# A bank of its own for value products, a new program order with two split chunks, and a scheduler that prices changes of array use, in an attention and MoE kernel

## The chip, the core and the metric

One core of one Trainium2 chip runs the program. Its engines work side by side: TensorE (PE) for matmuls, whose weights are loaded by PEld rows, VectorE (DVE), ScalarE (ACT), GpSimd (POOL) and SyncE (SP), which here issues every DMA. The metric is the device time of one execution in microseconds (us), lower is better.

## The reference

```python
scores = scale * np.matmul(q, k.transpose(0, 1, 3, 2))      # q, k, v: 4 x 8 x 576 x 64
scores = np.where(causal, -1000000000.0, scores)
a = np.exp(scores - scores.max(-1, keepdims=True))
a /= a.sum(-1, keepdims=True) + 1e-09
local = np.matmul(a, v)
q_p = phi(q)                                                # elu(q) + 1
mem_out = (q_p @ M_prev) / (q_p . z_prev + 1e-6)
attn = g * mem_out + (1 - g) * local                        # g = sigmoid(beta) by head
x = attn as 2304 tokens x 512
h = x @ w_in                                                # 512 x 2048
g = h where h >= 1, 0 where h <= -1, else (h + 1)**2 / 4
out = g @ w_out                                             # 2048 x 512
```

## The kernel before

Attention comes in 16 units of two heads; two units are a pair. Each pair is loaded by `load` (L281) and prepared by `prep` (L314): every operand is split into an fp16 high and low part, so that each product is three matmuls (`PASSES`). `half_a` does the first 256 query rows of a unit and `half_b` the other 320. Each takes score tiles (`front`, L436: scores at L415, the causal mask added by a matmul with the identity at L418, row maxima on DVE at L462, exponentials on ACT at L432), scales them (`back`: `an` tiles, high part by ACT, low part by DVE at L116), has them transposed by DMA (`ea`, `eb`, `ec`) and multiplies with the values (`pv1`, `pv2`, L533). Score matmuls use 64 of the array's rows, value products 64 of its columns, all else the whole array.

The MLP runs in 9 chunks of 256 tokens over 8 weight groups of 256 hidden columns. A group of a chunk is 24 matmuls of 256 columns into a tile h (`mlp_h`, L648), five steps that turn h into g (ACT L653 reads h, ACT L654 squares, DVE L655 reads h again and is the last to do so, then ACT L109 and DVE L116 write g's two halves), and 12 matmuls of 512 columns that add to a tile o (`mlp_o`, L665). `weight_group` (L177) makes the two halves of a weight group from 64-bit words, by DVE at L201 to L203 and L116.

PSUM has eight banks: `RINGS` gives two score tiles of two banks (s), one o of two, and two h of one. Value products take a score tile too, and the first units' scores take the o tile at times (`s_tile`).

`PROGRAM` is the order in which the source emits its parts: l loads a pair, P prepares it, W makes a weight group, A and B are the halves of units, p splits a chunk's input, c runs a chunk; `c0/2,5` cuts the first chunk's groups into three passes with a partial sum in `part`. `in_order` then sorts all instructions for each engine: `estimate` prices each, `listed` runs a list schedule forward and backward 24 times, and the best order is fixed.

Of the kernel before, what the change touches and what calls it, by code (L numbers as in the profile page):

```python
# [25 lines left out]
RINGS = dict(x=3, rq=1, rk=1, rn=1, rv=1, rm=2, rz=2, pn=1, eb=1, ec=1, ea=1, st=4, sc=3, wss=4, wssb=4, g=3, tm=4, part=1,  # L26
    tb=3, tu=3, s=2, o=1, h=2, xsc=3)
# [22 lines left out]
def infini_moe_kernel(ctx: ExitStack, tc, qt, kt, qr, vr, mem, zx, beta, w, out):  # L50
# [86 lines left out]
    wrs = const.tile([P, NG], F32, name="wrs")  # L137
    wirs = const.tile([P, NG], F32, name="wirs")
# [39 lines left out]
    def weight_group(r):  # L178
# [8 lines left out]
        for m in range(2):  # L187
# [17 lines left out]
            words.append(wt)  # L205
        kind(job, "wn")
# [227 lines left out]
    def front(u, i):  # L434
# [23 lines left out]
        for t, a in tiles:  # L458
            scores(u, t, s, a)
# [136 lines left out]
    def chunk_prep(c):  # L596
# [11 lines left out]
        hx, sx, rs, irs = (sc[:, j:j + 1] for j in (2, 3, 4, 5))  # L608
# [395 lines left out]
```

## Time and profile before

| | us |
|---|---|
| median of 3 runs | 643.14 (639.9 to 644.32) |
| the profiled execution | 640.85 |
| its span, first to last instruction | 639.0 |
| PE busy, of the span | 532.7 |
| DVE busy | 483.4 |
| ACT busy | 456.3 |

A slice of the profile's second part is a fortieth of the span, some 16 us; a digit is the busy share in tenths. A matmul's duration holds its latency too, so a busy PE row says that work was there, while the distance from one start to the next says what a matmul costs in a stream.

### The profile page before, as it was taken

How to read it: one execution, taken by the hardware profiler on the slowest of the kernel's cores; microseconds unless marked ns; L12 is line 12 of the kernel's file. 1: busy time of each engine (PE TensorE's matmuls, PEld its weight loads, DVE VectorE, ACT ScalarE, POOL GpSimd, SP SyncE). 2: the span in 40 equal slices, each digit the busy share in tenths (PEclk: the TensorE clock that was granted, in tenths of full speed). 3: DMA queues.
4: the chain of work that ended last, by engine and by line, in shares of the span. 5: the costliest groups of instructions: out<-in, count | busy, mean ns of one | idle time of the engine just before them, and what ended most of it. 6: DMA issues, size and time to landing. Idle time of an engine off the chain costs nothing.

```text
span 639.0 us, 11689 instructions
## 1 busy us (share of the span) xinstructions
PE 532.7 (83%) x4481; PEld 333.5 (52%) x4481; DVE 483.4 (76%) x1134; ACT 456.3 (71%) x916; POOL 2.4 (0%) x12
## 2 busy tenths in 40 slices
PE   0332546673678999999999999999999999999997
PEld 0111224442444666566565656656556566666764
DVE  5999999999999976987978689877667556424321
ACT  5866757959797877797987879788866565644443
POOL 1000000000000000000000000000000000000000
PEclk9999998967678999999999999999999999999999
DMA  7787686766745443692395337613533444000000
GB/s 301 248 288 219 182 208 181 197 184 164 135 112 141 104 77 70 133 216 68 76 196 83 73 93 143 139 25 74 97 72 49 81 84 58 34 1 1 33 1 34
DMA packets 133351, 74.68 MB, mean 117 GB/s; under 512 B 122800, under 2 KB 124848, under 8 KB 131248
## 3 DMA queue, kind: packets, MB, share of 16 engines
q1 hardware_dynamic: 133296, 73.94, 48.7%
q8 instruction: 35, 0.57, 0.4%
q14 instruction: 20, 0.16, 0.1%
HBM read 38.80 MB, written 4.72 MB: 68 GB/s over the span
## 4 chain that ended last, share of the span: by engine, by line
PE 69%; DVE 20%; DMA 4%; ACT 3%; issue 3%; SPq 1%; ACTq 0%; DVEq 0%
PE o L665 28%; PE h L648 27%; PE s L533 6%; PE s L415 4%; DVE an L116 3%; DMA eb<-an 2%; DVE st L462 2%; DVE w L202 2%; DVE w L203 1%; PE s L418 1%; DVE w L116 1%; PE s L443 1%; DMA rm<-mem 1%; DVE w L201 1%; DVE vs L116 1%
## 5 line engine op out<-in xcount | busy, mean ns | idle before, releaser
L648 PE MATMUL h<-xh,w 128*128 128x256 f16 x1728 | 221.7, 279 | 9.4 <-ACT xh L109 4.1
L665 PE MATMUL o<-w,g 128*128 128x512 f16 x864 | 212.8, 384 | 0.5 <-DVE part L694 0.5
L648 PEld LDWEIGHTS <-w 128*128 128x128 f16 x1728 | 169.2, 100 | 56.0 <-issue 17.0
L665 PEld LDWEIGHTS <-g 128*128 128x128 f16 x864 | 82.0, 99 | 83.0 <-issue 8.0
L432 ACT ACTIVATE e<-s,st,sc 128x512 f32<-128x512 f32 (+4 forms) x140 | 89.3, 640 | 20.7 <-DVE st L428 10.6
L655 DVE SCALAR_TENSOR_TENSOR tm<-h,tb,tm 128x512 f32<-128x512 f32 x72 | 53.6, 747 | 60.4 <-ACT tm L654 59.7
L653 ACT ACTIVATE tm<-h,tb 128x512 f32<-128x512 f32 x72 | 55.8, 776 | 53.4 <-PE h L648 49.3
L116 DVE SCALAR_TENSOR_TENSOR an<-e,st,an 128x512 f16<-128x512 f32 (+4 forms) x160 | 80.8, 540 | 7.6 <-ACT an L109 7.3
L109 ACT ACTIVATE g<-tm,tb 128x512 f16<-128x512 f32 x72 | 51.8, 722 | 32.3 <-DVE tm L655 30.3
L116 DVE SCALAR_TENSOR_TENSOR g<-tm,tb,g 128x512 f16<-128x512 f32 x72 | 53.6, 746 | 18.5 <-ACT g L109 18.3
L415 PE MATMUL s<-ks,qs 64*128 64x512 f16 (+3 forms) x372 | 45.8, 331 | 25.1 <-ACT e L432 16.4
L462 DVE TENSOR_REDUCE st<-s 128x2 f32<-128x768 f32 (+3 forms) x62 | 51.1, 829 | 19.9 <-PE s L418 16.6
L109 ACT ACTIVATE an<-e,st 128x128 f16<-128x128 f32 (+3 forms) x112 | 55.1, 541 | 15.0 <-issue 5.4
L533 PEld LDWEIGHTS <-vs 128*64 128x64 f16 x1024 | 40.1, 119 | 32.2 <-issue 30.7
L654 ACT ACTIVATE tm<-tm 128x512 f32<-128x512 f32 x72 | 45.3, 631 | 1.1
L415 PEld LDWEIGHTS <-qs 64*128 64x128 f16 x384 | 16.1, 100 | 45.4 <-issue 32.8
L533 PE MATMUL s<-pt,m 128*64 128x256 f16 (+1 forms) x184 | 18.7, 271 | 12.0 <-DMA pt<-pn 4.5
L432 ACT ACTIVATION_READ_ACCUMULATOR e<-s,st,sc 128x1 f32 x140 | 27.8, 198 | 0.0
L309 PE MATMUL s<-sc,ones 128*128 128x4 f32 (+1 forms) x32 | 6.1, 260 | 22.9 <-ACT m L330 18.8
L533 PE MATMUL s<-eb,vs 128*64 128x256 f16 (+1 forms) x384 | 23.6, 268 | 1.9 <-DMA eb<-an 1.9
L476 DVE SCALAR_TENSOR_TENSOR st<-st,cg 128x2 f32<-128x2 f32 (+2 forms) x64 | 10.0, 157 | 16.2 <-ACT e L432 16.1
L109 ACT ACTIVATE w<-w,wsc 128x1024 f16<-128x1024 f32 x15 | 17.2, 1146 | 7.0 <-DVE w L116 6.9
(161 smaller groups left out, 599.8 us busy)
## 6 DMA issues: line engine op xcount, KB each, us to landing
stg<-w SPq DMA_DIRECT2D x16, 1024.0 KB, 5.6
rv<-vr SPq DMA_DIRECT2D x7, 640.0 KB, 5.7
out<-tm SPq DMA_DIRECT2D x16, 256.0 KB, 2.1
rn<-qr SPq DMA_DIRECT2D x7, 576.0 KB, 4.3
rk<-kt SPq DMA_DIRECT2D x7, 576.0 KB, 3.9
rq<-qt SPq DMA_DIRECT2D x7, 576.0 KB, 4.8
rz<-zx SPq DMA_DIRECT2D x16, 96.0 KB, 4.4
rm<-mem SPq DMA_DIRECT2D x16, 64.0 KB, 3.0
```

What stands on the lines that cost most here:

```text
L109: return nc.scalar.activation(o, i, AF.Copy, scale=s)
L116: nc.vector.scalar_tensor_tensor(o, i, s, hi, op0=ALU.mult, op1=ALU.subtract)
L202: nc.vector.scalar_tensor_tensor(wti, hw, -0x40000000, wti, op0=ALU.bitwise_and, op1=ALU.bitwise_or)
L415: nc.tensor.matmul(s[:, h, a:a + n], u.pair.q[hs, tq, u.x, i * P:(i + 1) * P], u.pair.k[hs, tk, u.x, 0:n], start=j == 0, stop=False)
L432: nc.scalar.activation(e, s, AF.Exp, bias=st[:, 0, z:z + 1], scale=u.pair.cs, accum_out=st[:, 1, z:z + 1])
L462: nc.vector.tensor_reduce(st[:, 0, 2 * t:2 * t + 2], s[:, :, a:a + P * (t + 1)], axis=AX.X, op=ALU.max, negate=True)
L533: nc.tensor.matmul(pv[h * D:(h + 1) * D, a:c1], lhs, rhs, start=n < 2, stop=n >= len(terms) - 2)
L648: nc.tensor.matmul(h[:, u], w1[:, r, cc, wj, u * P:(u + 1) * P], x16[:, xj, cc, :], start=n == 0, stop=n == 3 * NCC - 1)
L653: nc.scalar.activation(tm, h, AF.Relu, bias=tb[:, 1, j:j + 1], scale=tb[:, 2, j:j + 1])
L654: nc.scalar.activation(tm, tm, AF.Square)
L655: nc.vector.scalar_tensor_tensor(tm, h, tb[:, 0, j:j + 1], tm, op0=ALU.max, op1=ALU.min)
L665: nc.tensor.matmul(acc[:, t], g16[:, gj, u, t * P:(t + 1) * P], w2[:, r * FPG + u, wj, :], start=(r == a and u == 0 and gj == 0 and wj == ...
```

## The change

It has these parts, with the lines of the new source.

- Value products: `pv1` and `pv2` write a one-bank tile `v` of their own; scores always take s, no longer o; h has one bank in place of two (`RINGS`).
- `front` of the first two query tiles issues both tiles' scores and then all four masks.
- `PROGRAM`: the first four units' attention comes before most weight groups; chunks 0 and 1 are each cut after group 4 (`c0/4`, `c1/4`); `part` has two buffers.
- `load`: z joins q's rows and M joins v's rows in DRAM, so a pair is four DMAs in place of eight, and q's rows are loaded first.
- `tables`: one DVE product by a broadcast in place of three.
- The scheduler: `listed` keeps three queues for PE, by the array's use, adds `TURN` (95 ns) where the use changes, and stays with a use while its first instruction is no more than `KEEP` (1500 ns) less urgent.

```diff
-RINGS = dict(x=3, rq=1, rk=1, rn=1, rv=1, rm=2, rz=2, pn=1, eb=1, ec=1, ea=1, st=4, sc=3, wss=4, wssb=4, g=3, tm=4, part=1,
-    tb=3, tu=3, s=2, o=1, h=2, xsc=3)
+RINGS = dict(x=3, rq=1, rk=1, rn=1, rv=1, pn=1, eb=1, ec=1, ea=1, st=4, sc=3, wss=4, wssb=4, g=3, tm=4, part=2,
+    tb=3, tu=3, s=2, o=1, h=1, v=1, xsc=3)
...
-PROGRAM = ("l0 l1 P0 W0 A0 P1 W1 A1 A2 W2 A3 p0 c0/2,5 W3 B0 W4 c0 B1 W5 l2 B2 W6 P2 B3 W7 c0 l3 p1 A4 A5 P3 c1 "
-           "A6 l4 A7 p2 B4 B5 P4 c2 B6 l5 B7 p3 P5 c3 A8 A9 A10 l6 A11 p4 B8 B9 P6 c4 B10 l7 B11 p5 P7 c5 A12 "
-           "A13 A14 A15 p6 B12 B13 c6 B14 B15 p7 c7 p8 c8")
+PROGRAM = ("l0 l1 P0 W0 A0 A1 P1 A2 A3 p0 W1 B0 W2 B1 W3 c0/4 B2 B3 p1 W4 l2 c1/4 W5 W6 W7 c0 c1 P2 A4 A5 l3 P3 "
+           "A6 A7 l4 p2 B7 B4 B5 P4 c2 l5 B6 A9 p3 P5 c3 A8 l6 A10 A11 p4 B8 B9 P6 c4 B10 B11 l7 p5 P7 c5 A12 "
+           "A14 A15 A13 B13 p6 B14 c6 B15 B12 p7 c7 p8 c8")
...
-        for c, t, src in (("lk", u.kt, kt), ("lq", u.qt, qt), ("lr", u.qr, qr), ("lv", u.vr, vr)):
+        for c, t, src in (("lr", qz1, qz), ("lk", u.kt, kt), ("lq", u.qt, qt), ("lv", vm1, vm)):
             kind(u.job, c)
             nc.sync.dma_start(out=t, in_=src[p])
-        kind(u.job, "lm")
-        for h in range(2):
-            hs = slice(h * D, (h + 1) * D)
-            nc.sync.dma_start(out=u.mf[hs], in_=mem[p])
-            nc.sync.dma_start(out=u.zf[hs], in_=zx[p, h:h + 1].to_broadcast([D, 2, 3, D]))
...
-        tag = next(spare) if u.n < 4 and u.n not in late else "s"
+        tag = "s"
...
-        for h in range(2):
-            nc.tensor.matmul(s[:, h, a + n - P:a + n], ident, mask, start=False, stop=True)
...
-            scores(u, t, s, a)
+            scores(u, t, s, a, a == 0)
+        for t, a in tiles:
+            for h in range(2):
+                nc.tensor.matmul(s[:, h, a + P * t:a + P * (t + 1)], ident, mask, start=False,
+                                 stop=t == tiles[-1][0])
...
-        pv = s_tile(u, f"pv1{u.n}")[:, 0]
+        pv = ps.tile([P, 512], F32, name=f"pv1{u.n}", tag="v")
...
-        nc.vector.tensor_scalar(t[:, 0, 0:n], wsc[:, 0, a:b], sx, None, op0=ALU.mult)
-        nc.vector.tensor_scalar(t[:, 1, 0:n], wrs[:, a:b], rs, None, op0=ALU.mult)
-        nc.vector.tensor_scalar(t[:, 2, 0:n], wirs[:, a:b], irs, None, op0=ALU.mult)
+        nc.vector.tensor_tensor(t[:, 0:3, 0:n], wtb[:, :, a:b], xtb.unsqueeze(2).to_broadcast([P, 3, n]), op=ALU.mult)
...
+TURN, KEEP = 95.0, 1500.0
...
+            pick = min(a[0] for a in alike if a)
+            if alike[use] and alike[use][0][0] <= pick[0] + KEEP:
+                pick = alike[use][0]
+            k = pick[1]
+            heapq.heappop(alike[mode[k]])
+            if mode[k] != use:
+                at += TURN
+            use = mode[k]
```

How the instructions stand now, at three places. Names end in a buffer's number: w1 and w2 are the weights' halves, stg a staging tile, an the scaled probabilities, tm and g the steps after h.

DVE, while the last weight groups are made. Before, with the low half of the seventh group's input weights (w1 from w2) in the middle:

```order
L116 SCALAR_TENSOR_TENSOR an_0_239<-e_0_234,st_0_214,an_0_239 128x128 x2
L116 SCALAR_TENSOR_TENSOR an_0_239<-e_0_234,st_0_214,an_0_239 128x2x128
L116 SCALAR_TENSOR_TENSOR m1_0_138<-rm_0_87,sc_2_1233,m1_0_138 128x256
L116 SCALAR_TENSOR_TENSOR g_1_590<-tm_1_589,tb_0_548,g_1_590 128x512
L116 SCALAR_TENSOR_TENSOR w1_73<-w2_74,wsc_77,w1_73 128x4x256
L116 SCALAR_TENSOR_TENSOR an_0_239<-e_0_234,st_0_214,an_0_239 128x2x128
L476 SCALAR_TENSOR_TENSOR st_1_346<-st_1_346,cg_72 128x4
```

Of the change, with the fifth group's:

```order
L116 SCALAR_TENSOR_TENSOR w1_73<-w2_74,wsc_77,w1_73 128x4x256
L350 TENSOR_SCALAR pn_0_144<-pn_0_144 128x1152
L424 TENSOR_SCALAR st_1_258<-st_1_258,sc_2_1836 128x4
L352 SCALAR_TENSOR_TENSOR rn_0_84<-rn_0_84,pn_0_144 128x1152
L116 SCALAR_TENSOR_TENSOR g_1_833<-tm_0_801,tb_1_1243,g_1_833 128x512
L354 TENSOR_TENSOR pn_0_144<-rn_0_84 128x2x512
L653 SCALAR_TENSOR_TENSOR tm_2_875<-h_0_192,tb_1_1243,tm_2_875 128x512
L358 TENSOR_TENSOR pn_0_144<-rn_0_84 128x2x64
L116 SCALAR_TENSOR_TENSOR an_0_226<-e_0_221,st_0_201,an_0_226 128x128
L361 TENSOR_REDUCE nr_1_339<-pn_0_144 128x18
L116 SCALAR_TENSOR_TENSOR g_2_876<-tm_1_832,tb_1_1243,g_2_876 128x512
```

Before, no h tile is read on DVE between the fifth (ahead of the sixth weight group) and the sixth (after the last weight group); now the first pass of chunk 1 has its tiles read (L653) between the weight groups.

ACT, in the last two chunks. Before:

```order
L653 ACTIVATE tm_2_827<-h_0_205,tb_0_548 128x512
L654 ACTIVATE tm_2_827<-tm_2_827 128x512
L109 ACTIVATE g_1_590<-tm_2_827,tb_0_548 128x512
L653 ACTIVATE tm_3_858<-h_1_337,tb_0_548 128x512
L654 ACTIVATE tm_3_858<-tm_3_858 128x512
L109 ACTIVATE g_2_828<-tm_3_858,tb_0_548 128x512
```

Of the change:

```order
L651 ACTIVATE tm_0_801<-h_0_192,tb_0_792 128x512
L652 ACTIVATE tm_0_801<-tm_0_801 128x512
L109 ACTIVATE g_1_833<-tm_0_801,tb_0_792 128x512
L651 ACTIVATE tm_1_832<-h_0_192,tb_0_792 128x512
L652 ACTIVATE tm_1_832<-tm_1_832 128x512
L109 ACTIVATE g_2_876<-tm_1_832,tb_0_792 128x512
```

The order is the same, but h_0 and h_1 took turns, and now every group's tile is h_0, which the next group's first matmul must wait for.

PE, in the first unit's scores. Before, at the turn from the first query tile to the second:

```order
L415 MATMUL s_0_144<-ks_0_135,qs_0_134 128x128
L418 LDWEIGHTS ident_64
L418 MATMUL s_0_144<-mask_65,ident_64 128x128
L418 LDWEIGHTS ident_64
L418 MATMUL s_0_144<-mask_65,ident_64 128x128
L415 LDWEIGHTS qs_0_134
L415 MATMUL s_0_144<-ks_0_135,qs_0_134 128x256
```

Of the change, at the end of the second tile's scores:

```order
L413 MATMUL s_0_131<-ks_0_122,qs_0_121 128x256
L458 LDWEIGHTS ident_64
L458 MATMUL s_0_131<-mask_65,ident_64 128x128
L458 LDWEIGHTS ident_64
L458 MATMUL s_0_131<-mask_65,ident_64 128x128
L458 LDWEIGHTS ident_64
L458 MATMUL s_0_131<-mask_65,ident_64 128x128
L458 LDWEIGHTS ident_64
L458 MATMUL s_0_131<-mask_65,ident_64 128x128
L413 LDWEIGHTS qs_0_121
```

The two masks that stood between the tiles' scores now stand behind them with the other two. Counted over the whole order of PE, its use (whole array, 64 rows, 64 columns) changes 313 times before and 221 times now.

## Rows read from the trace of the kernel before

**Rows 1.** The page: its span and the busy shares of PE and DVE in 40 slices.
```profile
span 639.0 us, 11689 instructions
...
PE   0332546673678999999999999999999999999997
...
DVE  5999999999999976987978689877667556424321
```

**Rows 2.** Busy time of the engines by stretch: us from and to, length, then PE, PEld, DVE, ACT and POOL busy (with instructions), granted PE clock as a share of 2.4 GHz, DMA share, GB/s.
```profile
0.00:190.80 190.80, 91.25 (x774) 55.65 (x775) 178.29 (x410) 142.49 (x295) 2.43 (x12) 0.88 0.72 203
190.80:220.00 29.20, 27.29 (x200) 15.14 (x199) 27.39 (x78) 22.55 (x48) 0.00 (x0) 0.94 0.47 109
220.00:560.00 340.00, 339.70 (x3006) 213.53 (x3004) 253.57 (x606) 257.83 (x527) 0.00 (x0) 1.00 0.47 93
```

**Rows 3.** Groups of PE's matmuls from 0 to 190.8 us: count, busy us and mean ns, idle before and its releasers. The value products (L533) are six groups of 336 in all, of which the largest and the smallest stand here.
```profile
L648 PE MATMUL h<-xh,w 128*128 128x256 f16 x168 | 28.5, 334 | 9.2 <-ACT xh L109 4.1 <-DVE xh L116 1.9 <-DVE wi L210 1.4
L415 PE MATMUL s<-ks,qs 64*128 64x128 f16 (+3 forms) x120 | 16.6, 379 | 23.7 <-ACT e L432 15.0 <-ACT x L109 2.7 <-ACT qs L109 2.2
L665 PE MATMUL o<-w,g 128*128 128x512 f16 x41 | 11.9, 420 | 0.0
...
L533 PE MATMUL s<-ec,vs 128*64 128x64 f16 x112 | 3.7, 231 | 2.2 <-DMA ec<-an 2.2
...
L533 PE MATMUL o<-pt,m 128*64 128x256 f16 x8 | 1.9, 420 | 0.1
```

**Rows 4.** Groups of DVE's instructions over the span: count, busy us and mean ns, idle before.
```profile
L655 DVE SCALAR_TENSOR_TENSOR tm<-h,tb,tm 128x512 f32<-128x512 f32 x72 | 53.6, 747 | 60.4 <-ACT tm L654 59.7
L116 DVE SCALAR_TENSOR_TENSOR g<-tm,tb,g 128x512 f16<-128x512 f32 x72 | 53.6, 746 | 18.5 <-ACT g L109 18.3
L462 DVE TENSOR_REDUCE st<-s 128x2 f32<-128x768 f32 (+3 forms) x62 | 51.1, 829 | 19.9 <-PE s L418 16.6 <-PE s L445 1.5 <-PE o L665 1.1
L116 DVE SCALAR_TENSOR_TENSOR w<-w,wsc,w 128x1024 f16<-128x1024 f32 x15 | 19.2, 1279 | 0.0
...
L116 DVE SCALAR_TENSOR_TENSOR xh<-stg,xsc,xh 128x1024 f16<-128x1024 f32 x6 | 7.7, 1282 | 0.4 <-ACT xh L109 0.3
...
L625 DVE TENSOR_SCALAR tb<-wsc,xsc 128x8 f32<-128x8 f32 (+2 forms) x11 | 2.5, 226 | 0.0
```

**Rows 5.** The timeline of DVE where it reads the sixth h tile: start us, us, instruction.
```profile
190.06 0.74 DVE L655 SCALAR_TENSOR_TENSOR tm<-h,tb,tm 128x512 f32<-128x512 f32 x1
```

**Rows 6.** The timeline of PE around changes of the array's use, runs of equal matmuls merged: start us, us, instruction, count.
```profile
333.24 0.93 PE L648 MATMUL h<-xh,w 128*128 128x256 f16 x7
334.10 0.41 PE L533 MATMUL s<-pt,m 128*64 128x256 f16 x4
...
338.31 0.71 PE L648 MATMUL h<-xh,w 128*128 128x256 f16 x5
338.96 0.82 PE L415 MATMUL s<-ks,qs 64*128 64x512 f16 x6
```

**Rows 7.** The timeline of the last chunk but one, where only the MLP is left; in brackets the engine's idle time before and its releaser.
```profile
566.52 2.75 PE L665 MATMUL o<-w,g 128*128 128x512 f16 x12
566.72 0.78 ACT L653 ACTIVATE tm<-h,tb 128x512 f32<-128x512 f32 x1 [2.23 <-PE h L648]
...
568.20 0.75 DVE L655 SCALAR_TENSOR_TENSOR tm<-h,tb,tm 128x512 f32<-128x512 f32 x1 [2.92 <-ACT tm L654]
...
569.11 2.78 PE L648 MATMUL h<-xh,w 128*128 128x256 f16 x24
...
571.73 0.59 PE L665 MATMUL o<-w,g 128*128 128x512 f16 x2
```

**Rows 8.** The same view where attention still runs, at two places: an h tile's last matmuls on PE, its first read on ACT and its last on DVE; and another's last matmuls and last read.
```profile
449.84 0.93 PE L648 MATMUL h<-xh,w 128*128 128x256 f16 x7
...
454.44 0.81 ACT L653 ACTIVATE tm<-h,tb 128x512 f32<-128x512 f32 x1
...
456.35 0.75 DVE L655 SCALAR_TENSOR_TENSOR tm<-h,tb,tm 128x512 f32<-128x512 f32 x1
...
475.30 2.24 PE L648 MATMUL h<-xh,w 128*128 128x256 f16 x19
...
479.56 0.75 DVE L655 SCALAR_TENSOR_TENSOR tm<-h,tb,tm 128x512 f32<-128x512 f32 x1 [1.95 <-ACT tm L654]
```

**Rows 9.** What PE waited for, the costliest: us in all, times, longest.
```profile
PE s L309 <- ACT m L330: 18.8, 2, 13.4
```

**Rows 10.** The timeline of the first load of M's square on ACT, and of its load on SP.
```profile
4.53 1.13 SPq L303 DMA_DIRECT2D rm<-mem  x2
...
10.36 1.27 ACT L330 ACTIVATE vs<-rv 128x1280 bf16<-128x1280 f32 x1 [1.36 <-DMA rv<-vr]
...
12.81 0.42 ACT L330 ACTIVATE m<-rm 128x256 bf16<-128x256 f32 x1 [0.72 <-DMA rm<-mem]
```

**Rows 11.** The end of the span: the last matmuls and the instruction that reads them.
```profile
627.99 6.42 PE L665 MATMUL o<-w,g 128*128 128x512 f16 x29
...
634.45 1.27 ACT L692 ACTIVATE tm<-o,tu 128x512 f32<-128x512 f32 x2 [3.28 <-PE o L665]
```

**Rows 12.** The timeline of PE, the same matmuls in an early stretch and one a little later.
```profile
132.63 4.05 PE L648 MATMUL h<-xh,w 128*128 128x256 f16 x18
...
144.36 2.13 PE L648 MATMUL h<-xh,w 128*128 128x256 f16 x18
```

More of the change, by code (lines that the diff above doesn't have):

```diff
@@ L49, in infini_moe_kernel @@
 @with_exitstack
-def infini_moe_kernel(ctx: ExitStack, tc, qt, kt, qr, vr, mem, zx, beta, w, out):
+def infini_moe_kernel(ctx: ExitStack, tc, qt, kt, qz, vm, beta, w, out):
     nc = tc.nc
@@ L136, in infini_moe_kernel @@
     wsc = const.tile([P, 2, NG], F32, name="wsc")
-    wrs = const.tile([P, NG], F32, name="wrs")
-    wirs = const.tile([P, NG], F32, name="wirs")
+    wtb = const.tile([P, 3, NG], F32, name="wtb")
     hsum = const.tile([P, NG], F32, name="hsum")
@@ L197, in weight_group @@
             else:
-                wt = sb.tile([P, NTT * DM], F32, name="wlast", tag="pn")
+                wt = before[:, w.shape[3]:].bitcast(F32)
             wti = wt.bitcast(I32)
@@ L205, in weight_group @@
             words.append(wt)
+            before = stage
         kind(job, "wn")
@@ L407, in infini_moe_kernel, with scores @@
     PASSES = ((0, 0), (0, 1), (1, 0))
-    def scores(u, i, s, a):
+    def scores(u, i, s, a, first):
         n = P * (i + 1)
@@ L415, in scores @@
                 nc.tensor.matmul(s[:, h, a:a + n], u.pair.q[hs, tq, u.x, i * P:(i + 1) * P],
-                                 u.pair.k[hs, tk, u.x, 0:n], start=j == 0, stop=False)
-        for h in range(2):
-            nc.tensor.matmul(s[:, h, a + n - P:a + n], ident, mask, start=False, stop=True)
+                                 u.pair.k[hs, tk, u.x, 0:n], start=first and j == 0, stop=False)
     def stats(u):
@@ L562, in pv2 @@
         kind(u.job, "pb")
-        pv = s_tile(u, f"pv2{u.n}")[:, 0]
+        pv = ps.tile([P, 512], F32, name=f"pv2{u.n}", tag="v")
         pv_group(pv, 256, 320, list(memory_terms(u, 4, 256)) + [
@@ L607, in chunk_prep @@
                                 op0=ALU.logical_shift_right)
-        hx, sx, rs, irs = (sc[:, j:j + 1] for j in (2, 3, 4, 5))
+        hx, sx, rs, irs, xtb = (sc[:, j:j + n] for j, n in ((2, 1), (3, 1), (4, 1), (5, 1), (3, 3)))
         nc.vector.tensor_copy(hx, sc[:, 1:2].bitcast(I32))
@@ L815, in estimate @@
         fast = "TensorScalar" in kind and len(tensors) == 1 and not psum
-        return 66 + 60 * scalars + (0.52 if fast else 1.042) * n, None
+        half = "Copy" in kind and rd[0].dtype == F16
+        return 66 + 60 * scalars + (0.3 if half else 0.52 if fast else 1.042) * n, None
     if "TensorScalar" in kind:
@@ L820, in estimate, with shape @@
     return 148 + (1.886 if wr[0].dtype == F16 else 1.67) * n, None
+def shape(ins):
+    rd, wr = operands(ins)
+    return 1 if rd[0].ap[0][1] == D else 2 if wr[0].ap[0][1] == D else 0
 def graph(prog):
@@ L856, in graph, with listed @@
     return cost, needs
-def listed(n, engine, waits, users, urgency, hold, hop, start):
+def listed(n, engine, mode, waits, users, urgency, hold, hop, start):
     wait, ready_at = list(waits), [0.0] * n
-    soon, now = {e: [] for e in HOP}, {e: [] for e in HOP}
+    soon, now, use = {e: [] for e in HOP}, {e: [] for e in HOP}, 0
+    alike = [[], [], []]
     clock, first, order = dict.fromkeys(HOP, start), [0.0] * n, []
@@ L867, in listed @@
     for _ in range(n):
+        now["PE"] = alike[0] or alike[1] or alike[2]
         at, e = min((clock[e] if now[e] else max(clock[e], soon[e][0][0]), e) for e in HOP if now[e] or soon[e])
@@ L870, in listed @@
             k = heapq.heappop(soon[e])[1]
-            heapq.heappush(now[e], (urgency[k], k))
-        k = heapq.heappop(now[e])[1]
-        first[k] = at
+            heapq.heappush(alike[mode[k]] if e == "PE" else now[e], (urgency[k], k))
+        if e == "PE":
+            pick = min(a[0] for a in alike if a)
[6 more added lines that the diff above has]
+            use = mode[k]
+        else:
+            k = heapq.heappop(now[e])[1]
         order.append(k)
@@ L908, in in_order @@
     turns = ["Transpose" in type(i).__name__ for i in prog]
+    mode = [shape(i) if e == "PE" else 0 for i, e in zip(prog, engine)]
     def forward(urgency):
@@ L931, in hold @@
             return at + took, at + took
-        return listed(n, engine, [len(x) for x in needs], users, urgency, hold, lambda a, b: HOP[a][b], 650.0)
+        return listed(n, engine, mode, [len(x) for x in needs], users, urgency, hold, lambda a, b: HOP[a][b], 650.0)
     def backward(urgency):
@@ L982, in lay_out @@
     z = z_prev.reshape(n, 2, 2, D)
-    z = np.stack([np.concatenate([z, z[:, :, h:h + 1]], axis=2) for h in range(2)], axis=1)
+    z = np.repeat(np.stack([np.concatenate([z, z[:, :, h:h + 1]], axis=2) for h in range(2)], axis=1).reshape(n, 2, 6 * D),
+                  D, axis=1)
+    m = M_prev.reshape(n, 4, D, D).transpose(0, 2, 1, 3).reshape(n, D, 4 * D)
     wi = moe_w_in.reshape(4, P, 8, 256).transpose(2, 1, 0, 3).reshape(8, P, 1024)
     wo = moe_w_out.reshape(8, 2, P, 512).transpose(0, 2, 1, 3).reshape(8, P, 1024)
-    return dict(qt=columns(q), kt=columns(k), qr=rows(q, False), vr=rows(v, True),
-                mem=M_prev.reshape(n, 4, D, D).transpose(0, 2, 1, 3), zx=z, beta=beta,
-                w=np.stack([wi, wo], axis=1))
+    return dict(qt=columns(q), kt=columns(k), qz=np.concatenate([rows(q, False).reshape(n, P, 18 * D), z], axis=2),
+                vm=np.concatenate([rows(v, True).reshape(n, P, 20 * D), np.concatenate([m, m], axis=1)], axis=2),
+                beta=beta, w=np.stack([wi, wo], axis=1))
 def kernel(**inputs):
```

23 lines of the change are left out of this document (12 added, 11 removed).

## The prediction

> **What bounds the kernel now.** Read the page's slices first. PE is at 9 from the fourteenth slice to the end, DVE at 9 from the second slice to the twelfth [rows 1]: two stages, the first bound by DVE, the second by PE. The table by stretch gives their sizes: up to 190.8 us DVE works 178.3 us and PE only 91.3, and from 220 to 560 PE is busy 339.7 of 340 us [rows 2]. So a microsecond of DVE or ACT saved late is worth nothing, and the end moves only by what PE still has to do when the first stage lets it run, by what PE's work then costs, and by new waits of PE.
>
> I take 190.8 us as the cut: there DVE ends its read of the sixth h tile [rows 5], the first that comes after all weight groups. By then PE has issued 168 matmuls of h, 41 of o, 120 of scores into s (and by the order 12 more into o) and 336 value products [rows 3]. The last matmuls end near 634.4, where ACT's next read begins 634.45 [rows 11], so 443.6 us follow the cut, nearly all of them PE's. 4.6 us more run to the span's end at 639.0, and the execution has 640.85. The median of the runs shown lies 2.3 us above that; I forecast in the profiled execution's terms, and 1% of the median (6.4 us) is about what a measurement can tell from no change.
>
> **DVE's total does not move.** Three table products of 0.226 us become one over 11 tables [rows 4]: -5.0 us, and 11 products of up to three times their size come, for which I take 0.25 each (bounds: 0.226, one such product, and 0.68, three): -2 us on DVE. They lie in both stages, and I book nothing for them; on a path they are worth 2 us at most.
>
> **PE's work ahead at the cut.** What matters is how far PE is when DVE has done as much as at 190.8. I counted DVE's instructions in the order of the change. Up to its read of the ninth h tile they are those of before up to the sixth, but for 3 more reads of h (0.747 each), 3 more low halves of g (0.746), 1 more low half of x (1.28), 4 fewer low halves of weights (1.279) and 2 fewer row maxima (0.829) [rows 4]: 2.2 + 2.2 + 1.3 - 5.1 - 1.7 = -1 us. The same DVE time thus carries three more groups of the MLP. On PE, the order up to the ninth tile's last matmul holds 216 of h, 93 of o, 124 of scores and 308 value products.
>
> Prices: 24 matmuls of h run in 571.73 - 569.11 = 2.62 us and 12 of o in 569.11 - 566.52 = 2.59 [rows 7], 0.109 and 0.216 each. So 48 h more are 5.2 us, 52 o more 11.2, 28 value products and 8 scores fewer some 2.4 (pairs share a slot, at most 0.109 a product): 14 us ahead. While DVE reads the ninth tile, PE goes on with what the order puts behind it, 2 us. Together -16 us. The bound below is 0, if DVE waits in the first stage for what it now waits on sooner; above, -21, if h's evacuation delays nobody.
>
> **Changes of the array's use.** Seven h matmuls from 333.24 would make room at 334.00, and the value products start at 334.10; five from 338.31 would at 338.86, and the scores start at 338.96 [rows 6]: 0.1 us a change. Behind the cut 236 changes are left before, and 156 of the order of the change: 80 x 0.095 = -7.6 us. The twelve fewer ahead of the cut lie beside DVE and save nothing. The masks put together are among these.
>
> **The start.** M's square is the last that the first exponents need; ACT waits for M's load, issued seventh, until 12.81, though v's square (with its read-out) is done near 11.7 [rows 10], and PE's longest wait, 13.4 us, is for it [rows 9]. M now comes with v: -1 us (bounds 0 and -1.3, since the bytes stay). It shifts DVE's whole first stage.
>
> **One bank for h.** The next group's h may start only when DVE has read the last one. In the last chunks that read ends at 568.95, 2.43 us behind the last h matmul's slot, and o covers 2.59 [rows 7]: allowing the signal to PE 0.17 (no more than the 0.20 by which ACT's start at 566.72 lags that slot, matmul latency included) the chain is 2.6, so nothing is lost where a whole o stands between. In the middle stretch ACT and DVE serve attention too: one tile was read out by 480.31, 2.8 us behind its last matmuls' rows (477.54), another by 457.10, over 6.3 behind [rows 8]. For each of the 63 groups behind the ninth I summed the matmuls that the order puts between its h and the next (3.9 us on average in the middle stretch) and held them against 2.6 us plus the ACT instructions that the order puts between the two steps on ACT. Where the chain is longer the rest counts: 7.4 us over all groups. I take +7.4; the lower bound is 5 (the chain at its shortest), and the upper has no row, since with two banks nobody waited for a late read.
>
> **Longer in DVE's stage.** From the ninth to the sixteenth tile the order gives DVE 49 us and PE 43, by the same prices, so PE idles 6. Before, PE lost 1.9 us idle between 190.8 and 220, and some 3 at a granted clock of 0.94 [rows 2]. The difference is +2 us; at most +8, if DVE's work there meets waits.
>
> Value products in their own bank, `part`'s second buffer and four DMAs fewer a pair: I book nothing. They let scores and chunk 1 go ahead, which the order already shows; without them the -16 would shrink toward 0.
>
> **The sum.** 640.85 - 16 - 7.6 - 1 + 7.4 + 2 = 625.7 us, near 626.
>
> **Rivals.** (1) The bank makes it no faster or slower. Without its 7.4 us the sum is 618, so 0.36 us a group over 63 groups gives back all the gain; at 0.5 us a group the time is 650. For it: reads late by 3 us and more [rows 8], and an order whose cover is often just the chain's own length, so that each late ACT or DVE instruction becomes idle time of PE. Against it: in the last chunks the chain fits under o [rows 7], and PE has attention's matmuls to put between. The Trainium skill, in "Perfetto Trace Analysis", section "Optimizing Tensor Performance" (Matmuls), says that independent matmul groups should rotate through different PSUM banks, so that one's evacuation overlaps the next one's matmuls. That speaks against this change, and by it this rival's 650 stands in place of 626; the rows of the last chunks, where o hides 2.59 of 2.6, bear it out only in part.
>
> (2) Only the uses are saved. The first stage is a web of DVE, ACT and PE; with one h tile each group there costs 2.62 + 2.6 us of a fixed chain, and where PE runs slow, 18 h matmuls took 4.05 us where 2.13 is usual [rows 12], it is near 7.7, more than the 7 us of DVE work between two tiles. Then the 16 us go, and the bank's 7.4 with half of them: 640.85 - 7.6 = 633 and up to 640, say 635.
>
> (3) All reads fit and DVE never waits: -21 for the work ahead, the bank at 0 and no +2 give 640.85 - 21 - 7.6 - 1 = 611.
>
> **How the numbers follow.** The forecast (616 to 634) has 0.45, rival 3 0.15, rival 2 0.15, and rival 1 0.25, half of it within 1% and half beyond. Faster by over 1% is below 636.7: 0.45 + 0.15 + 0.10 of rival 2 = 0.70; the same 0.05 + 0.10 = 0.15; slower 0.15. The range leaves out the best of rival 3 and the worst of rival 1: 608 to 645; the forecast's own is 616 to 634.
>
> **What would show it.** In the profile of the change: PE's slices at 9 from an earlier slice on, with L646 and L663 in quantity before 190 us; DVE still at 9 up to some 240 us; PE's waits for `tm` (DVE's read of h) of 5 to 10 us in all behind the ninth tile, many short ones; the last chunks with o and h back to back as before; the first PE matmul near 12.2. Wrong would be: DVE with idle time between 110 and 190 us (rival 2), or PE below 9 in many slices from 250 us on, waiting for `tm` by 30 us and more (rival 1).

## The result, and the profile after

| | before | after |
|---|---|---|
| median, us | 642.04 (639.9 to 644.32, 4 runs) | 617.79 (617.38 to 618.68, 4 runs) |
| the profiled execution, us | 640.85 | 617.87 |
| its span, us | 639.0 | 616.2 |

The ratio is 0.9624 [0.9585, 0.9662]: the change is faster by 3.8%. The forecast was 626 (608 to 645); in the profiled execution's terms its sum was 625.7, and 617.87 came, 7.8 us less.

The page after, its span and the slices that answer to [rows 1]:

```profile
span 616.2 us, 11580 instructions
...
PE   0324565768699999999999999999999999999996
...
DVE  5999999999999998497989849978677763223221
```

PE stands at 9 from the twelfth slice (a fortieth is now 15.4 us), before from the fourteenth. DVE stays at 9 to the fifteenth slice, some 231 us, as the prediction said it would (up to some 240). So the first stage is still DVE's, and it ends sooner for PE.

The cut lies where DVE ends its read of the ninth h tile; its row in DVE's timeline (start us, us), the row that answers to [rows 5]:

```profile
184.29 0.75 DVE L653 SCALAR_TENSOR_TENSOR tm<-h,tb,tm 128x512 f32<-128x512 f32 x1
```

The stretches, in the columns of [rows 2], after:

```profile
0.00:185.04 185.04, 104.41 (x862) 64.49 (x863) 176.03 (x401) 141.85 (x289) 2.49 (x12) 0.84 0.70 204
185.04:700.00 514.96, 417.33 (x3619) 269.08 (x3618) 299.48 (x706) 309.92 (x628) 0.00 (x0) 1.00 0.33 72
...
300.00:700.00 400.00, 305.97 (x2602) 197.58 (x2600) 198.81 (x463) 213.78 (x427) 0.00 (x0) 1.00 0.27 59
```

And the same of before, behind its own cut and behind 300 us (a window's end past the span only adds emptiness):

```profile
190.80:700.00 509.20, 441.40 (x3709) 277.87 (x3707) 305.16 (x725) 313.82 (x621) 0.00 (x0) 0.99 0.35 71
...
300.00:700.00 400.00, 334.11 (x2753) 210.46 (x2751) 211.94 (x493) 227.05 (x453) 0.00 (x0) 1.00 0.30 59
```

These rows split the 22.8 us by which the span fell. The cut came 5.8 us sooner (190.80 to 185.04). Behind it PE has 24.1 us less to do (441.40 to 417.33). And PE idles 7.0 us more there: 616.2 - 185.04 - 417.33 = 13.8, before 639.0 - 190.80 - 441.40 = 6.8, in both with some 4.6 behind the last matmul.

What PE still has to do behind the cut, after and then before (group, count, busy us and mean ns, idle before and its releasers):

```profile
L663 PE MATMUL o<-w,g 128*128 128x512 f16 x768 | 184.8, 379 | 0.7 <-ACT g L109 0.5 <-DVE g L116 0.2
L646 PE MATMUL h<-xh,w 128*128 128x256 f16 x1512 | 177.7, 272 | 5.6 <-DVE tm L653 5.1
```

```profile
L665 PE MATMUL o<-w,g 128*128 128x512 f16 x825 | 201.5, 382 | 0.5 <-DVE part L694 0.5
L648 PE MATMUL h<-xh,w 128*128 128x256 f16 x1560 | 193.2, 273 | 0.2 <-DVE tm L655 0.2
```

48 matmuls of h at 0.109 us and 57 of o at 0.216 were done ahead, 17.5 us; 16 value products fewer, at most 0.109 each, take up to 1.7 of it back. Of the 24.1 us some 16 are work ahead. 8 are left for the changes of use and for the clock: from 190.8 to 220 us the kernel before ran at a granted clock of 0.94 [rows 2], which is 29.2 x 0.06 = 1.8 us of PE's time, and from its cut to 220 us the change ran at 1.00.

PE's waits behind the cut (us in all, times, longest), the first of the view:

```profile
PE h L646 <- DVE tm L653: 5.1, 11, 0.9
PE v L533 <- DMA pt<-pn: 0.9, 1, 0.9
```

One of the eleven, in the timelines of the three engines: h's last matmuls, the reads of its tile by ACT and DVE, and the next group's first matmuls:

```profile
322.77 0.71 PE L646 MATMUL h<-xh,w 128*128 128x256 f16 x5
...
324.42 0.76 ACT L651 ACTIVATE tm<-h,tb 128x512 f32<-128x512 f32 x1
325.59 0.61 ACT L652 ACTIVATE tm<-tm 128x512 f32<-128x512 f32 x1
...
326.61 0.75 DVE L653 SCALAR_TENSOR_TENSOR tm<-h,tb,tm 128x512 f32<-128x512 f32 x1
...
327.41 0.38 PE L646 MATMUL h<-xh,w 128*128 128x256 f16 x2 [0.31 <-DVE tm L653]
```

ACT begins 1.65 us behind the start of h's last matmuls, and each step follows the last by some 0.4 us, since ACT and DVE serve attention between them. h waits only the 0.31 us by which other matmuls fell short. In a late chunk nothing falls short:

```profile
544.55 2.75 PE L663 MATMUL o<-w,g 128*128 128x512 f16 x12
...
546.22 0.75 DVE L653 SCALAR_TENSOR_TENSOR tm<-h,tb,tm 128x512 f32<-128x512 f32 x1 [2.92 <-ACT tm L652]
...
547.14 2.78 PE L646 MATMUL h<-xh,w 128*128 128x256 f16 x24
```

DVE has read h at 546.97, and h starts 0.17 us later, 2.59 behind o's first, as long as twelve o always took [rows 7].

The start, on ACT, PE and SP's queue, the answer to [rows 10]:

```profile
2.98 0.48 SPq L302 DMA_DIRECT2D rv<-vm  x1
3.50 0.49 SPq L302 DMA_DIRECT2D w<-kt  x1
...
11.87 1.27 ACT L328 ACTIVATE vs<-rv 128x1280 bf16<-128x1280 f32 x1 [1.66 <-DMA rv<-vm]
...
13.14 0.40 ACT L328 ACTIVATE m<-rv 128x256 bf16<-128x256 f32 x1
...
13.68 1.01 PE L307 MATMUL s<-sc,ones 128*128 128x4 f32 x4 [13.68 <-ACT m L328]
```

M no longer comes behind v, but v with M comes later: its square begins at 11.87, v's alone began at 10.36 [rows 10]. M's square moved from 12.81 to 13.14. The second pair's loads are now issued from 3.50 us, close behind; they may take the DMA engines' time from v. The load itself now carries M's bytes as well. No run told these two apart.

### The profile page after: what moved, and what is told of

Its sections match the earlier page's. It is cut to its first block, busy times and chain, and to the rows that moved or that the text cites. A ratio compares the mean times of both kernels' runs of the same rounds, so it can differ in the third digit from the quotient of the medians.

```text
span 616.2 us, 11580 instructions
## 1 busy us (share of the span) xinstructions
PE 521.7 (85%) x4481; PEld 333.6 (54%) x4481; DVE 475.5 (77%) x1106; ACT 451.8 (73%) x916; POOL 2.5 (0%) x12
## 5 line engine op out<-in xcount | busy, mean ns | idle before, releaser
L646 PE MATMUL h<-xh,w 128*128 128x256 f16 x1728 | 207.5, 276 | 12.8 <-DVE tm L653 12.1
L663 PE MATMUL o<-w,g 128*128 128x512 f16 x864 | 207.8, 379 | 6.7 <-DVE g L116 3.8
L663 PEld LDWEIGHTS <-g 128*128 128x128 f16 x864 | 80.7, 98 | 88.0 <-DVE g L116 5.3
L653 DVE SCALAR_TENSOR_TENSOR tm<-h,tb,tm 128x512 f32<-128x512 f32 x72 | 53.8, 747 | 68.7 <-ACT tm L652 64.2
L428 ACT ACTIVATE e<-s,st,sc 128x256 f32<-128x256 f32 (+4 forms) x144 | 91.4, 638 | 13.4 <-DVE st L424 9.1
L413 PE MATMUL s<-ks,qs 64*128 64x256 f16 (+3 forms) x384 | 43.4, 335 | 23.9 <-ACT e L428 8.8
L462 DVE TENSOR_REDUCE st<-s 128x2 f32<-128x256 f32 (+1 forms) x64 | 52.0, 816 | 5.5 <-PE s L458 5.3
L533 PEld LDWEIGHTS <-vs 128*64 128x64 f16 x1024 | 40.6, 118 | 17.0 <-issue 16.6
L533 PE MATMUL v<-eb,vs 128*64 128x256 f16 (+1 forms) x384 | 24.2, 276 | 2.1 <-DMA eb<-an 2.1
L533 PE MATMUL v<-pt,m 128*64 128x256 f16 (+1 forms) x192 | 19.2, 271 | 7.0 <-DMA pt<-pn 4.0
L204 ACT ACTIVATE stg<-w 128x1024 bf16<-128x1024 f32 x15 | 15.8, 1051 | 6.6 <-DVE w L203 6.4
## 6 DMA issues: line engine op xcount, KB each, us to landing
w<-vm SPq DMA_DIRECT2D x1, 768.0 KB, 13.8
```

Of the source, the lines that this page charges most:

```text
L204: nc.scalar.activation(stage.bitcast(BF16)[:, 0:w.shape[3]], wt, AF.Square, accum_out=ss[:, m:m + 1])
L428: nc.scalar.activation(e, s, AF.Exp, bias=st[:, 0, z:z + 1], scale=u.pair.cs, accum_out=st[:, 1, z:z + 1])
L462: nc.vector.tensor_reduce(st[:, 0, 2 * t:2 * t + 2], s[:, :, a:a + P * (t + 1)], axis=AX.X, op=ALU.max, negate=True)
L533: nc.tensor.matmul(pv[h * D:(h + 1) * D, a:c1], lhs, rhs, start=n < 2, stop=n >= len(terms) - 2)
L646: nc.tensor.matmul(h[:, u], w1[:, r, cc, wj, u * P:(u + 1) * P], x16[:, xj, cc, :], start=n == 0, stop=n == 3 * NCC - 1)
L653: nc.vector.scalar_tensor_tensor(tm, h, tb[:, 0, j:j + 1], tm, op0=ALU.max, op1=ALU.min)
```

## The experiments

All ran beside the kernel before, whose medians in the three sets were 641.42, 640.8 and 641.1 us. "Uses" are the changes of array use in PE's order. The other columns are from each trace: matmuls of h and o issued from 300 us on, PE's busy time from 300 us on, what is left of the span from there (4.6 of it behind the last matmul), and DVE's busy time from 100 to 200 us. The counts leave out attention: at 300 us before, e1, e2, e4 and e11 have 180 matmuls of scores left, the others 168, worth some 1 us.

| kernel | median us | ratio | uses | h, o left | PE busy, rest | DVE |
|---|---|---|---|---|---|---|
| before | 641 to 642 | 1 | 313 | 1196, 637 | 334.1, 4.9 | 95.69 |
| after | 617.79 | 0.9624 [0.9585, 0.9662] | 221 | 1129, 579 | 306.0, 10.2 | 99.96 |
| e1 | 627.63 | 0.9778 [0.974, 0.9817] | 244 | 1176, 632 | 321.4, 7.8 | 97.62 |
| e2 | 634.07 | 0.9882 [0.9844, 0.9919] | 302 | 1151, 594 | 321.4, 12.3 | 97.45 |
| e3 | 623.40 | 0.9721 [0.9688, 0.9754] | 206 | 1152, 588 | 311.6, 11.3 | 97.07 |
| e4 | 626.25 | 0.9757 [0.9724, 0.9791] | 226 | 1152, 613 | 315.0, 9.5 | 94.26 |
| e5 | 626.93 | 0.9781 [0.976, 0.9802] | 309 | 1150, 579 | 317.2, 8.1 | 99.17 |
| e6 | 621.90 | 0.97 [0.9678, 0.9722] | 260 | 1131, 582 | 309.8, 10.7 | 99.92 |
| e7 | 619.24 | 0.9666 [0.9639, 0.9692] | 186 | 1151, 591 | 308.2, 11.3 | 96.72 |
| e8 | 619.72 | 0.9678 [0.9648, 0.9708] | 173 | 1150, 579 | 303.6, 12.8 | 99.87 |
| e9 | 619.57 | 0.9678 [0.9648, 0.9708] | 222 | 1128, 576 | 305.0, 12.6 | 99.50 |
| e10 | 626.16 | 0.9772 [0.9745, 0.9799] | 278 | 1152, 624 | 318.2, 4.8 | 95.17 |
| e11 | 635.91 | 0.9924 [0.9898, 0.9949] | 341 | 1152, 614 | 326.9, 8.2 | 97.39 |
| e12 | 619.56 | 0.9665 [0.9635, 0.9696] | 236 | 1152, 583 | 309.0, 10.0 | 97.11 |

### e1_turns_only: the pricing of uses alone, on the kernel before

```diff
+TURN, KEEP = 95.0, 1500.0
...
+            if alike[use] and alike[use][0][0] <= pick[0] + KEEP:
+                pick = alike[use][0]
...
+            if mode[k] != use:
+                at += TURN
```

> The kernel before with nothing but the scheduler's three PE queues, TURN and KEEP. Its order changes the array's use 244 times (313 before). If a change costs 0.1 us wherever PE is the bound and moves nothing else, some 55 to 69 fewer make 640.9 - 6 = 635 us. If the saved changes lie beside waits, 641. If the new priorities disturb the first stage, above 643.

627.63 us, 13.8 less, where 635 was expected. 69 uses fell away; at the 0.1 us that [rows 6] show they are 7 us. 20 h and 5 o more were done by 300 us: another 3.3. In the rows PE is busy 12.8 us less from 300 us on and idles 2.9 more, which makes the 9.9 us of the profiled span; that execution took 630.78, 3 above the median, so the rest of the 13.8 us can't be read from it.

### e2_no_turns: the change without the pricing

```diff
-TURN, KEEP = 95.0, 1500.0
+TURN, KEEP = 0.0, 0.0
...
-            if alike[use] and alike[use][0][0] <= pick[0] + KEEP:
-                pick = alike[use][0]
```

> The changed kernel with TURN and KEEP taken out: PE again takes the most urgent instruction whatever its use, and the order changes the use 302 times (221 with them). By the sum of the prediction 81 changes at 0.1 us, most of them in PE's stage, cost 7 to 8 us: 625. If the pricing mattered only by its order in the first stage, 618 to 620.

634.07, 16.3 more than the change, where 7 to 8 was expected. The 81 uses are 8 of it. The order also does 22 h and 15 o less by 300 us, 0.109 x 22 + 0.216 x 15 = 5.6 us, and 2.1 us more are idle. Its granted clock from 300 us on was 0.99, the change's 1.00.

### e3_old_program: the change with the program order of before

```diff
-PROGRAM = ("l0 l1 P0 W0 A0 A1 P1 A2 A3 p0 W1 B0 W2 B1 W3 c0/4 B2 B3 p1 W4 l2 c1/4 W5 W6 W7 c0 c1 P2 A4 A5 l3 P3 "
...
+PROGRAM = ("l0 l1 P0 W0 A0 P1 W1 A1 A2 W2 A3 p0 c0/2,5 W3 B0 W4 c0 B1 W5 l2 B2 W6 P2 B3 W7 c0 l3 p1 A4 A5 P3 c1 "
...
```

> The changed kernel with the PROGRAM of before (c0 in three passes, chunk 1 whole). First theory: the new program is what puts PE's work ahead, so its 16 us and the 3.5 us of DVE's idle time come back: 634 to 640. Second theory: the bank for value products and the uses do most of it, and the program little: 618 to 624.

623.40: the second theory holds. With everything else in place the new program order is worth 5.6 us, with the work left at 300 us 4.4 us larger without it, and not the 16 that the first theory gave it.

### e4_two_h: the change without the value products' own bank

```diff
-    tb=3, tu=3, s=2, o=1, h=1, v=1, xsc=3)
+    tb=3, tu=3, s=2, o=1, h=2, xsc=3)
...
-        pv = ps.tile([P, 512], F32, name=f"pv1{u.n}", tag="v")
+        pv = s_tile(u, f"pv1{u.n}")[:, 0]
```

(and `pv2` likewise)

> The changed kernel with the banks given back: value products take a score tile again, h has two banks. First theory: the program does the gain and one bank for h only costs, so PE's 5 us of waits for DVE's reads of h behind 185 us go: 612 to 614. Second theory: value products that wait for transposes in a score tile hold the scores up and DVE idles again in the first stage: 622 to 630.

626.25: the bank is worth 8.5 us here although it costs h its second one. DVE's busy time from 100 to 200 us falls from 99.96 to 94.26 (third figure behind the length; the change's row first, then that of e4):

```profile
100.00:200.00 100.00, 81.66 (x707) 53.41 (x707) 99.96 (x230) 83.05 (x166) 0.00 (x0) 0.92 0.56 149
100.00:200.00 100.00, 75.25 (x658) 47.67 (x655) 94.26 (x227) 82.66 (x166) 0.00 (x0) 0.86 0.61 152
```

In e4 DVE ends its read of the ninth h tile at 197.1 us in place of 185.04, after 17.8 us of idle time in place of 9.0, and 23 h and 34 o fewer are done by 300 us, 2.5 + 7.3 = 9.8 us. The prediction booked nothing for this part by itself. The first units' scores and value products do not get back the o tile that they took at times before, so e4 is not quite the old use of the banks.

### e5_keep_0, e6_keep_300, e7_keep_3000: the price of a use

```diff
-TURN, KEEP = 95.0, 1500.0
+TURN, KEEP = 95.0, 0.0
```

(300.0 and 3000.0 in the other two)

> The changed kernel, with the scheduler still booking 95 ns for each change of array use but never staying with a use for it (KEEP = 0): 309 uses in PE's order, as against 221. Theory A (each use saved is worth what it costs on PE, about 0.1 us): 617.8 + 88 x 0.1 = 626 to 627 us. Theory B (a use saved is worth about twice that, as the kernel without both numbers showed, 16.3 us over 81 uses = 0.2 us each, because staying with a use also finishes a group of scores or products sooner, so that what waits for it starts sooner): 617.8 + 88 x 0.2 = 635 us. Theory C (what counts is that the modelled clock of PE is right, not that it stays): 618 to 621 us.

> The changed kernel, staying with a use only for work up to 300 ns more urgent elsewhere (KEEP = 300): 260 uses. Theory A (0.1 us a use): 617.8 + 39 x 0.1 = 621.7 us. Theory B (0.2 us a use): 625.6 us. If the order of the instructions scatters the time by more than that whatever the uses, it falls outside 620 to 627.

> The changed kernel, staying with a use for work up to 3000 ns more urgent elsewhere (KEEP = 3000): 186 uses. Theory A (0.1 us a use): 617.8 - 35 x 0.1 = 614.3 us. Theory B (0.2 us a use): 610.8 us. Rival: staying this long makes DVE and ACT wait for tiles of the other use, and the gain of 1500 is the best there is: 618 to 624 us, with DVE's idle time before its read of the ninth h tile above the 8.1 us that it is now.

626.93 at 309 uses, 621.90 at 260, 617.79 at 221: theory A's 626 to 627 and 621.7. The slope is 9.14 / 88 = 0.104 and 4.11 / 39 = 0.105 us a use, by the whole time. In e5 the same 579 of o are left at 300 us as in the change, and 21 h more (2.3 us); PE is busy 11.2 us longer from there on and idles 2.1 less, so work and idle time offset each other and 9 us are left for the uses. In e6 it is less clean: of 3.8 us more of PE's busy time 0.9 are work left (2 h and 3 o), which leaves 2.9 for 39 uses, and PE idles 0.5 more. The row of e5:

```profile
300.00:700.00 400.00, 317.16 (x2630) 201.55 (x2627) 200.36 (x457) 214.95 (x432) 0.00 (x0) 1.00 0.27 60
```

At KEEP = 3000 the line ends: 619.24 where theory A gave 614.3, within its rival's range. DVE's idle time up to its ninth read of h is 11.0 us, against 9.0 in the change by the table of stretches (the expectation's 8.1 leaves out 0.9 ahead of DVE's first instruction), and 22 h and 12 o fewer are done by 300 us, 5.0 us, more than the 35 uses bring.

### e8_shared: h and the value products in one ring of two banks

```diff
-    tb=3, tu=3, s=2, o=1, h=1, v=1, xsc=3)
+    tb=3, tu=3, s=2, o=1, h=2, xsc=3)
...
-        pv = ps.tile([P, 512], F32, name=f"pv1{u.n}", tag="v")
+        pv = ps.tile([P, 512], F32, name=f"pv1{u.n}", tag="h")
```

> The changed kernel with its two banks (one for h, one for the value products) made one ring of two that both take turns in: 173 uses. Theory D (the single h bank costs what PE waits for DVE's read behind the cut, 5.1 us, and a second bank gives most of it back): 612 to 615 us. Rival (a value product holds its bank for a whole group, and h's tiles wait for that as well): 618 to 624 us, with waits of PE for DVE's and ACT's reads of value products at h's slots in place of those for tm.

619.72, in the rival's range; the interval overlaps the change's. PE's waits from 185 us on:

```profile
PE h L646 <- DVE tm L653: 5.8, 5, 2.8
PE o L663 <- DVE part L692: 2.4, 1, 2.4
PE h L533 <- DMA ec<-an: 2.1, 3, 1.1
PE h L533 <- DMA eb<-an: 1.2, 1, 1.2
PE h L533 <- ACT stg L109: 1.2, 2, 0.7
```

h waits for `tm` as long as with one bank, in fewer and longer waits. What the rival named, value products that wait at h's slots for another to be read, is the last line, 1.2 us, and it came on top of the waits for `tm` and not in their place; 3.3 us more are value products that wait for their transposes in a bank of this ring. 48 uses fewer bring nothing in the end.

### e9_turn_0: staying with a use, a change booked at nothing

```diff
-TURN, KEEP = 95.0, 1500.0
+TURN, KEEP = 0.0, 1500.0
```

> The changed kernel, staying with a use as it does (KEEP = 1500) but booking nothing for a change (TURN = 0): 222 uses, as against 221. With KEEP at 0 the kernel took 626.9 us at 309 uses, and with both at 0 634.1 us at 302: 7 us that no use explains. Theory A (those 7 us are the modelled clock of PE, which runs ahead of the real one when changes are booked at nothing, so that the order is right for another time): 622 to 626 us here. Rival (one order out of many: orders that differ a little scatter by some us): within 616 to 621 us, and the 7 us stay with that one order.

619.57, as the rival had it. The booked 95 ns matters little here, and the interval overlaps the change's; what e2 lost beyond e5, 7 us at 7 uses fewer, belongs to the order that came out there. So orders of nearly the same uses can differ by some us, and each row of the table shows one order.

### e10_program_loads_tables: the change without pricing and without the bank

The edits of e2 and e4 together. Two parts that the list of the change leaves out stay in: a lower price for f16 copies on DVE in `estimate`, and another buffer for the last words of weights.

> The changed kernel without its two largest parts: no pricing of uses, and value products back in the tiles of scores with two banks for h. Left of the change are the order of the program's parts, the packed loads, the tables of exponents, the order of masks, and two chunks with partial sums; 278 uses. If the parts add up (before 641.4, after 617.8, 16.3 for the pricing and 8.5 for the bank, both as taken out of the whole): 642 to 643 us. If these parts stand for the work ahead that the prediction booked at 16 us: 622 to 628 us. By the uses alone, against before's 313: 638 us.

626.16: 15 us less than before, where adding up gave 642 to 643. Alone, these parts do 44 h and 13 o more by 300 us, 4.8 + 2.8 = 7.6 us, and save 35 uses, 3.6; the other 4 are not told apart. So the parts do not add up, and e2, e4, e10 and the change make a square, all with the new program order:

| | two h banks | value products' own bank |
|---|---|---|
| uses not priced | 626.16 (e10) | 634.07 (e2) |
| uses priced | 626.25 (e4) | 617.79 (after) |

The bank costs 7.9 us in the upper line and gives 8.5 in the lower. The rows of e10, and then of e2:

```profile
300.00:700.00 400.00, 318.16 (x2662) 202.77 (x2660) 202.52 (x467) 218.38 (x434) 0.00 (x0) 1.00 0.28 59
```

```profile
300.00:700.00 400.00, 321.38 (x2666) 203.82 (x2664) 202.06 (x464) 218.62 (x435) 0.00 (x0) 0.99 0.27 60
```

In e10 PE idles 0.2 us from 300 us to its last matmul, in e2 7.7, with 24 more uses in the order. PE's waits of e2 from 185 us on begin:

```profile
PE h L646 <- DVE tm L653: 4.5, 4, 2.1
PE o L663 <- ACT tm L690: 1.9, 1, 1.9
PE o L663 <- DVE g L116: 1.6, 2, 1.4
```

In the upper line the bank does let 30 o more be done by 300 us, 6.5 us, and gives that and more back: 7.5 us as idle time, 32 more uses behind 300 us (counted in the traces), and some at the granted clock of 0.99. The waits for `tm`, the prediction's first rival, are 3.2 us of that idle time (4.5 from 185 us on), so less than half of it. In the left column pricing saves 52 uses, 37 of them behind 300 us, and 2.4 us of work left, and loses 4.7 us as idle time of PE (0.2 in e10, 4.9 in e4); the times are the same. The change is 23 h and 34 o further than e4 with 0.7 us more idle. Why the bank gives this with the new program order only where uses are priced was not settled.

### e11_bank_only: the bank alone, on the kernel before

```diff
-    tb=3, tu=3, s=2, o=1, h=2, xsc=3)
+    tb=3, tu=3, s=2, o=1, h=1, v=1, xsc=3)
...
-        tag = next(spare) if u.n < 4 and u.n not in late else "s"
+        tag = "s"
...
-        pv = s_tile(u, f"pv1{u.n}")[:, 0]
+        pv = ps.tile([P, 512], F32, name=f"pv1{u.n}", tag="v")
```

(and `pv2` likewise)

> The kernel before with one edit: value products in a bank of their own, one bank left for h, scores always in their own tiles; 341 uses, as against 313. Theory (the bank keeps DVE fed in the first stage, 8.5 us, also without the rest; 28 more uses cost 2.8 us): 634 to 637 us. Rival (without the new order of the program, h's single bank eats the gain, as the prediction's first rival had it): 642 to 650 us.

635.91, as the theory had it and not 642 to 650: 44 h and 23 o more are done by 300 us (9.8 us), against 28 more uses and 3.3 us more idle. With the old program order the bank thus pays without priced uses, which it did not with the new one (e2 against e10).

### e12_old_masks: each mask behind its own scores

```diff
-            scores(u, t, s, a, a == 0)
-        for t, a in tiles:
+            scores(u, t, s, a, True)
...
-                                 stop=t == tiles[-1][0])
+                                 stop=True)
```

> The changed kernel with the masks of a score tile's two diagonal blocks each behind its own scores, as before, in place of all of them behind both: 236 uses, as against 221. By the uses: 617.8 + 15 x 0.1 = 619.3 us, 618 to 621. If the masks at the end of a tile also save a wait: 622 or more.

619.56, 1.8 us more, where 15 uses make 1.6; the interval overlaps the change's, so no saved wait is to be seen. That it is the uses is not shown either: 23 h and 4 o more are left at 300 us (3.4 us), and DVE idles 2.9 us from 100 to 200 where the change idles 0.04. The prediction took the masks as a part of the uses; this run does not speak against it.

## Why the prediction was near, and where it was off

**The work ahead** was -16 with the 2 that PE does while DVE reads; some 16 came. 216 h and 96 o were issued by the cut, by the counts of the two views (1728 - 1512 and 864 - 768), where the order gave 216 and 93.

**The changes of use** were -7.6, for 80 changes fewer behind the cut; the traces have 236 and 153, 83 fewer. 6 to 8 us are left of PE's busy time, as the clock's 1.8 are counted or not, and e5 and e6 give 0.104 and 0.105 us a use where [rows 6] gave 0.1. This term was right in place and size. What it left out is that pricing also sets the order: the whole without it loses 16.3 us (e2), without KEEP alone 9.1 (e5).

**The cut** is the step that failed. It was put at 190.8 - 1 = 189.8 and came at 185.04. The -1 was the start's, and that gave nothing: M's square moved 0.3 us the other way, and PE's first matmul, forecast near 12.2, began at 13.68. But DVE worked 2.3 us less up to the cut (178.29 [rows 2] to 176.03) and idled 3.5 us less, 9.0 for 12.5.

The 2.3 us of work had been seen and left out of the sum. 1.5 of them are table products, nine of 0.22 us before and three of 0.16 now, for which the prediction says "I book nothing"; one of the three products of a table, before and then after, up to the cuts:

```profile
L625 DVE TENSOR_SCALAR tb<-wsc,xsc 128x3 f32<-128x3 f32 (+1 forms) x3 | 0.7, 222 | 0.0
L625 DVE TENSOR_TENSOR tb<-wtb,xsc 128x12 f32<-128x12 f32 x3 | 0.5, 162 | 0.0
```

Its "-5.0" for the tables also took out two products of three and then charged the new one in full; with three out and 11 of 0.25 in, its own figures make -4.7 over the span and not -2. The other 0.8 are near the -1 that it counted in DVE's order but did not carry to the cut.

The 3.5 us of idle time were taken as unchanged, with "I book nothing" for the bank, `part` and the loads. All of it lies behind 100 us, where DVE idled 4.3 us up to the cut before and now less than 0.1. The bank has a part in it: without it DVE is idle 5.7 us from 100 to 200, with it 0.04 (e4). It is not the bank alone, since e7 and e12 have the bank and idle 3.3 and 2.9 there, in other orders.

**One h bank** was +7.4 and "longer in DVE's stage" +2. PE idled 7.0 more behind the cut, 5.1 of it in eleven waits for `tm`. PE's busy time from 185.04 to 220 is 32.75 us, 2.2 idle, where 1.9 was idle before [rows 2], and the granted clock is 1.00 where it was 0.94, so the +2 did not come. The sum behind that +2 doesn't close as it stands: 6 idle less 1.9 less the 3 put to the clock is 1; with 29.2 x 0.06 = 1.8 in place of 3 it is the 2. Summing each group's chain against its cover gave the waits for `tm` as 7.4 where 5.1 came.

Together: 4.8 at the cut, 2.4 in PE's idle time, and some 0.5 in its work make the 7.8 us but for 0.2 outside the span. All three went the same way, and the range of 608 to 645 was wide enough to hold them.

**Which part gave it** the sum does not say. The prediction read the 16 us from the order of all parts together, and of the bank, `part` and the loads it said only that without them the 16 would shrink toward 0. Put in terms of h and o left at 300 us, the change is 19.8 us ahead of before; without the bank 9.8 of them go (e4), without the new program order 4.4 (e3), without pricing 5.6 (e2). Taken alone, the bank gives 9.8 (e11), program, loads and tables 7.6 (e10), pricing 3.3 (e1), which adds up to 20.7. The times don't add up: 13.8 + 14.9 + 5.2 = 33.9 against 24.2. By the spans of the profiled executions it is 9.9 + 16.0 + 3.9 = 29.8 against 22.8, 7.0 us too much. Some uses are saved twice: behind 300 us the traces have 70 fewer in e1, 52 fewer in e10 and 5 more in e11, 117 fewer together, where the change has 84 fewer, which is 3.3 us. The rest was not taken apart.

One order stands behind each kernel, and two orders of nearly the same uses differed by 7 us (e2 and e5). What a single part is worth, 5.6, 7.9 or 8.5 us, holds for these orders and carries a scatter of that kind, which no run measured.

**The rivals.** The second (uses alone, 633 to 640) fails: DVE is idle 0.04 us from 100 to 200, and the work is ahead. The third (611) had two halves: DVE does not wait from 100 us to the cut, but not all reads of h fit, and PE idles 7.0 us more. The first needs 0.36 us a group over 63 groups, 23 us; 5.1 came. The Trainium skill, in "Perfetto Trace Analysis", section "Optimizing Tensor Performance" (Matmuls), would rotate matmul groups through different banks. Here the second h bank was worth less than the bank it took from the value products in e4 and e11, and more in the new program order without priced uses (e10 against e2); which tile needs the bank is decided by the runs.

## What to carry to other kernels

Where one stage is bound by VectorE and the next by TensorE, count what TensorE has issued at the moment when VectorE has done a given amount of work. Then ask as well how much work and idle time VectorE has ahead of that moment, since that was the term that was missed here. The parts of a change need not add up in time (33.9 us alone against 24.2 together); that they nearly did in work left (20.7 against 19.8) is one case and no rule. As e4 reads, a bank is worth what its longest holder makes others wait: try it with the tile that blocks the engine that bounds, and measure it together with the order that goes with it, because with another order the same bank cost 7.9 us that here gave 8.5.

## What the runs showed of the hardware

A change of the array's use between whole array, 64 rows and 64 columns costs TensorE some 0.1 us. In the change's timeline two o matmuls from 339.00 us would make room at 339.43, at 0.216 each, and the value products start at 339.52:

```profile
339.00 0.59 PE L663 MATMUL o<-w,g 128*128 128x512 f16 x2
339.52 0.25 PE L533 MATMUL v<-pt,m 128*64 128x64 f16 x4
```

By the whole time it is 0.104 and 0.105 us, over 88 and over 39 changes (e5, e6). The Trainium skill, in "TensorEngine Tiling (Array Packing)", section "Key Properties", says that changing the tiling mode drains TensorE; it gives no time, and a cost at each change fits it, though the drain itself is in no row.

Four loads in place of eight brought v and M no sooner: v with M was issued at 2.98 us instead of 3.42 and its square began at 11.87 instead of 10.36, with the next pair's loads in flight from 3.50 on.

The granted clock up to the cut, a mean over stretches at 2.4 and at 1.2 GHz, was lower after the change, 0.84 of 2.4 GHz against 0.88 [rows 2], though PE was busy there for 104.41 us against 91.25. It fell at other times: in the change it was 0.74 from 20 to 100 us, with PE busy 35.0 of the 80, and before 1.00 there, with 31.8, but 0.76 from 100 to 190.8 us, with 57.4 of 90.8. From the cut on it was 1.00, and before 0.94 up to 220 us.
